# A three-layer float32 kernel: the first half batch of layer 1 multiplied with whole float32 W1out and g, their splits made later

## The chip, the core and the metric

The kernel runs on one NeuronCore of a Trainium2 chip. Its engines are called here as the profile calls them: PE (TensorE, matrix multiplications into PSUM), DVE (VectorE), ACT (ScalarE), POOL (GpSimd), SP (SyncE, which issues most of the DMA transfers). The metric is the device time of one execution in microseconds (us); lower is better.

## The reference

An approximate attention (Nystrom, 32 landmarks) feeds two gated layers; 4 batches of 576 tokens, 8 heads of 64, model width 512, inner width 2048. The weights are float64 arrays, q, k and v are float32.

```python
def _attn_ref(q, k, v):
    q_lm = q.reshape(B, H, m, S // m, D).mean(axis=3)
    k_lm = k.reshape(B, H, m, S // m, D).mean(axis=3)
    A = sm(q, k_lm)
    Bm = sm(q_lm, k_lm)
    C = sm(q_lm, k)
    Z = Bm.transpose(0, 1, 3, 2) / (norm1(Bm) * norm_inf(Bm) + 1e-06)
    for _ in range(6):
        Z = 2 * Z - Z @ Bm @ Z
    return A @ Z @ C @ v

def _moe_ref(x, w_in, w_out):
    h = x @ w_in
    g = h - np.tanh(h)
    return g @ w_out

def _moe2_ref(x, w_in, w_out):
    h = x @ w_in
    g = h * np.tanh(softplus(h))
    return g @ w_out

x = attention, heads side by side       # 2304 x 512
x = _moe_ref(x, moe_w_in, moe_w_out)
x = _moe2_ref(x, moe2_w_in, moe2_w_out)
```

## The kernel before, in words

**Products.** To keep float32 precision, an operand is kept as two float32r tiles: H, the value rounded by a copy on ACT, and L, what is left, by a subtraction on DVE or POOL (`split`). A product is then three multiplications: H with H, L with H, H with L. The attention's small products (`blocks`, `heads`) use whole float32 tiles, with several small tiles side by side in PE's array.

**Converting the weights.** A weight tile of 128x512 float64 values is loaded as 128x512x2 32-bit words into a ring of four buffers, `raw`. `f32_a` makes from the upper words a float32 y on ACT (sign, exponent and upper bits of the fraction) and moves the lower words right by 29 bits: on ACT by a Copy with a scale, or on DVE by a shift (`on_act` chooses). `f32_b` puts both together on DVE (scalar_tensor_tensor). `convert(jobs, act_share)` runs a list of such jobs as a generator, with the loads three tiles ahead; tile i shifts on ACT where i % act_share is 0. Before, the first call has act_share 1: always ACT. `keep_job` leaves a W1in tile whole (and stores it to DRAM for the later batches); `split_job` splits a tile into a buffer of `wo_p`: 16 buffers of 128x2x512, for the 16 tiles f of W1out, later of W2out.

**Slots.** Layer 1 runs over 128 slots s = 32 b + 16 hf + f: batch b, half hf of its 576 tokens (288 columns), tile f of the inner width. In `slot(s)`, `h1` makes h in PSUM by six multiplications (P, which is W1in with the attention's landmark part multiplied in by `p_gen`, times AT, the attention's left factor). `vec` takes h through ACT and DVE: s, th, q on ACT, the mask mk, products g and th, and the steps `small` and `pick` (copy_predicated) of the slot before, which finish g. Two slots later `vec` splits that g into gg (H on ACT, L on DVE or POOL). `y1` of slot s - 3 (LAG = 3) adds to four PSUM tiles y with 12 multiplications, 6 of them ahead of the background work (`bg`) and 6 behind it. After f = 15 the y tiles go out through ACT.

`E()` names the engine for the mask and the L parts: DVE, but POOL in slots 24 to 103. A scheduler orders the instructions of slots below 116 (SWITCH), with higher priority for marked ones; from there they stand as written. In the slots of batch 0, `cv` converts the rest of the first layer's weights, `p_gen` makes the next P, and `attn_all(1)` prepares the next batch. The second layer follows in 96 slots with `h2` and `o2`; its gg ring has five buffers.

Of the kernel before, what the change touches and what calls it, by code (L numbers as in the profile page):

```python
# [8 lines left out]
F32 = mybir.dt.float32  # L9
F32R = mybir.dt.float32r  # L10
# [4 lines left out]
ALU = mybir.AluOpType  # L15
# [12 lines left out]
def kernel(  # L28
# [18 lines left out]
    NF = 16  # L47
# [4 lines left out]
    PAIR = 26  # L52
    NPRE = 9
    PREP = 16
    SWITCH = 116
    C2 = 384
    NC2 = NT // C2
# [2 lines left out]

    dram = ctx.enter_context(tc.tile_pool(name="dram", bufs=1, space=DRAM))
    const = ctx.enter_context(tc.tile_pool(name="const", bufs=1))
    wo_p = ctx.enter_context(tc.tile_pool(name="wo", bufs=NF))
    st_p = ctx.enter_context(tc.tile_pool(name="st", bufs=4))
    raw_p = ctx.enter_context(tc.tile_pool(name="raw", bufs=4))
    ps_y = ctx.enter_context(tc.tile_pool(name="ps_y", bufs=4, space=PSUM))
# [24 lines left out]
    def E():  # L91

        return G if 24 <= cur[0] < NS - 24 else V

    def f32(ap):
        return ap.bitcast(F32)
# [59 lines left out]
    def split_job(src, pool, tag, dst, i):  # L156
        def done(y):
            w = pool.tile([128, 2, 512], F32R, tag=tag, name=tag)
            split(y, w[:, 0, :], w[:, 1, :], E())
            dst[i] = w  # L160
        return src, done, None

    def keep_job(src, g, j, a):
        def where():
# [11 lines left out]
    def convert(jobs, act_share=1, more=None):  # L176
        n = len(jobs)
        raws, st, los = {}, {}, {}
        ahead = 4 if more else 3

        def fetch(i):
            if i < n:
                raws[i] = load_raw(jobs[i][0], more if more and i % 6 > 3 else None)

        for i in range(ahead):
            fetch(i)
        for i in range(n + 2):
            if i < n:
                st[i], *los[i] = f32_a(raws.pop(i), i % act_share == 0)
            if i - 1 in los:  # L190
                where = jobs[i - 1][2]
                yield from f32_b(st[i - 1], *los.pop(i - 1), where() if where else st[i - 1])
            fetch(i + ahead)
            if i >= 2:
                jobs[i - 2][1](st.pop(i - 2))
            yield 1
# [345 lines left out]

    def vec(s):
        new, old = [], []
        if 2 <= s < NS + 2:
            with tc.high_priority(20):
                g2 = sv[s - 2][0]
                gg = tp[0].tile([128, 2, HS], F32R, tag="gg", name="gg")
                split(g2, gg[:, 0, :], gg[:, 1, :], E())
                sv[s - 2] = gg  # L550
        if s == NS:
            A.preload_act_table_set("mish")
            tables["prelu"] = False
        if s < NT_S:
            h = hp.pop(s)
            if s < NS:
                e = tmp(s, "s")
                t = tmp(s, "th")
                g = tmp(s, "g", 4)
                q = tmp(s, "q")  # L560
                mk = t1_p.tile([128, HS], U8, tag="mk", name="mk")
                A.activation(out=e, in_=h, func=ACTF.Square)  # L562
                A.activation(out=t, in_=h, func=ACTF.Tanh)  # L563
                with tc.high_priority(40):
                    A.activation(out=q, in_=e, func=ACTF.Exp, scale=FK)

                def mask_op(eng):
                    eng.tensor_scalar(out=mk, in0=e, scalar1=FT, scalar2=None, op0=ALU.is_ge)  # L568

                if E() is G:  # L570
                    mask_op(G)
                new = [
                    lambda: E() is G or mask_op(V),
                    lambda: V.tensor_tensor(out=g, in0=h, in1=e, op=ALU.mult),  # L574
                    lambda: V.tensor_tensor(out=t, in0=h, in1=t, op=ALU.subtract),
                ]
                with tc.high_priority(40):
                    A.activation(out=q, in_=q, func=ACTF.Square, scale=FB, bias=bias_c[:, 0:1])  # L578
                sv[s] = (g, t, q, mk)
            else:  # L580
                g = tp[1].tile([128, C2], F32, tag="g", name="g")
                gg = tp[1].tile([128, 2, C2], F32R, tag="gg", name="gg", bufs=5)
                A.activation(out=gg[:, 0, :], in_=h, func=ACTF.Mish)  # L583
                A.activation(out=g, in_=h, func=ACTF.Mish)  # L584
                new = [lambda: V.tensor_tensor(out=gg[:, 1, :], in0=g, in1=f32(gg[:, 0, :]), op=ALU.subtract)]  # L585
                sv[s] = gg
        if 1 <= s <= NS:
            g0, t0, q0, mk0 = sv[s - 1]

            def small():  # L590
                with tc.high_priority(40):
                    V.tensor_tensor(out=g0, in0=q0, in1=g0, op=ALU.mult)

            def pick():
                with tc.high_priority(40):
                    V.copy_predicated(out=g0, mask=mk0, data=t0)  # L596

            old = [small, pick]
        while old or new:
            for lst in (old, new):  # L600
                if lst:
                    lst.pop(0)()
                    yield 0
        yield 1

    def y1(s, half):
        f = s % 16
        gg = sv[s]
        w = W1o[f]
        for d in (2 * half, 2 * half + 1):  # L610
            if f == 0:
                yps[d] = ps_y.tile([128, 512], F32, tag="y", name="y")[:, 0:HS]
            c = slice(128 * d, 128 * d + 128)
            mm(yps[d], w[:, 0, c], gg[:, 0, :], start=(f == 0), stop=False)  # L614
            mm(yps[d], w[:, 1, c], gg[:, 0, :], start=False, stop=False)  # L615
        for d in (2 * half, 2 * half + 1):
            c = slice(128 * d, 128 * d + 128)
            mm(yps[d], w[:, 0, c], gg[:, 1, :], start=False, stop=(f == NF - 1))  # L618
        if f == NF - 1:
            o = raw_f32()[:, 0:2 * HS].rearrange("p (d n) -> p d n", d=2)  # L620
            for d in range(2):
                A.activation(out=o[:, d], in_=yps[2 * half + d], func=ACTF.Copy)
            nc.sync.dma_start(out=ys[s // 16][:, 2 * half:2 * half + 2], in_=o)
# [66 lines left out]
    def vec_only(g, rate=[1]):  # L690
        while True:
            yield 1
            n = 0
            for x in g:
                n += x
                if n == rate[0]:
                    break
                yield 0
            else:
                return  # L700
            yield 1
# [42 lines left out]
    if True:  # L744
# [5 lines left out]
            return [keep_job(w1i[j, g, a], g, j, a) for g in range(NG) for a in range(2)]  # L750

        def wo_jobs(src, dst, lo, hi):
            return [split_job(src[i], wo_p, "w", dst, i) for i in range(lo, hi)]

        jobs = w1i_jobs(0) + wo_jobs(w1o, W1o, 0, NPRE)
        rest = [(4 * j, n) for j in (1, 2, 3) for n in w1i_jobs(j)]
        rest += [(f + LAG, n) for f, n in zip(range(NPRE, NF), wo_jobs(w1o, W1o, NPRE, NF))]
        jobs += [x[1] for x in sorted(rest, key=lambda x: x[0])]
        rate = [1]
        cv = vec_only(convert(jobs), rate)  # L760
        pre = hi(attn_pre(0), 60)
        pa = both(attn_a, 0, 0, True)
        n = nc_ = 0
# [44 lines left out]
        def bg(s):  # L808
            b, i = s // 32, s % 32
            streams, mix = [], []  # L810
            if b == 0:
                rate[0] = 2 if i < 4 else 1
                mix.append(cv)
                while ready and i:
                    streams.append(p_gen(0, ready.pop(0)))
            if s < NS:
# [97 lines left out]
```

## Time and profile before

| what | value |
| --- | --- |
| median of 3 runs | 851.7 us (851.68 to 852.64) |
| the profiled execution | 851.59 us |
| its span in the trace | 849.8 us, 15003 instructions |
| busy, PE | 812.7 us (96%) |
| busy, DVE | 503.3 us (59%) |
| busy, ACT | 496.6 us (58%) |
| busy, POOL | 179.0 us (21%) |
| moved by DMA | 79.62 MB |

Busy shares are means over the whole span; the profile's page also has them in 40 slices of 21 us. Matmuls are pipelined, and a record lasts longer than the distance to the next: what one costs in a row of them is read from start to start. "<-" behind an idle time names what ended it. A float32 multiplication gives two records.

### The profile page before, as it was taken

The numbers are of one execution on the slowest core, as the hardware profiler recorded it, in microseconds if no ns is written. First come the engines' busy times: TensorE is split into PE (matmuls) and PEld (weight loads), VectorE is DVE, ScalarE is ACT, GpSimd is POOL, SyncE is SP. The second block draws the span as 40 slices with busy tenths as digits, with TensorE's granted clock in tenths as the row PEclk, the third lists the DMA queues.
The fourth block names the chain that finished last, engine by engine and source line by source line (L and its number), as shares of the span: only waits on it lengthen the run. The fifth ranks groups of instructions, "written<-read, shape, count | busy, mean of one in ns | idle before, by whom it ended". The sixth has DMA issues, their size and how long they took to land.

```text
span 849.8 us, 15003 instructions
## 1 busy us (share of the span) xinstructions
PE 812.7 (96%) x5656; PEld 706.5 (83%) x5656; DVE 503.3 (59%) x1158; ACT 496.6 (58%) x1234; POOL 179.0 (21%) x210
## 2 busy tenths in 40 slices
PE   4599899999999999999999999999999999999998
PEld 1346689889988899879899999999999999999996
DVE  6878999998789877999973986322111111211111
ACT  5888976788778886799874865333223222222221
POOL 0010003886577666870000000000000000000000
PEclk9557999999999999999999999999999999999999
DMA  9899240430415100360006662022002001000000
GB/s 327 289 338 366 105 136 6 148 136 1 141 51 183 51 30 1 119 215 20 29 2 225 202 195 69 1 66 74 1 1 66 10 1 49 18 1 9 30 1 37
DMA packets 34985, 79.62 MB, mean 94 GB/s; under 512 B 5472, under 2 KB 14176, under 8 KB 34912
## 3 DMA queue, kind: packets, MB, share of 16 engines
q1 hardware_dynamic: 33760, 74.46, 26.0%
q0 software_dynamic: 1152, 4.19, 1.2%
q8 instruction: 44, 0.72, 0.4%
q14 instruction: 29, 0.24, 0.1%
HBM read 65.01 MB, written 13.63 MB: 93 GB/s over the span
## 4 chain that ended last, share of the span: by engine, by line
PE 74%; DVE 12%; ACT 5%; POOL 3%; DMA 2%; issue 2%; SPq 0%; DVEq 0%; ACTq 0%
PE y L642 7%; PE y L638 7%; PE y L637 7%; PE y L614 6%; PE h L537 5%; PE h L536 5%; PE h L535 5%; PE y L618 5%; PE y L615 5%; PE m L211 3%; PE m L537 2%; PE h L511 2%; PE m L536 2%; PE m L535 2%; DVE g L596 2%; PE h L513 2%
## 5 line engine op out<-in xcount | busy, mean ns | idle before, releaser
L585 DVE TENSOR_TENSOR gg<-g,gg 128x384 fp32r<-128x384 f32 x96 | 53.5, 558 | 276.0 <-ACT g L584 276.0
L614 PE MATMUL y<-gg,w 128*128 128x288 f32 x512 | 151.3, 310 | 5.4 <-ACT gg L99 4.1
L615 PE MATMUL y<-gg,w 128*128 128x288 f32 x512 | 143.8, 296 | 0.0
L614 PEld LDWEIGHTS y<-gg,w 128*128 128x128 f32 x512 | 97.0, 189 | 29.4 <-issue 15.3
L618 PE MATMUL y<-gg,w 128*128 128x288 f32 x512 | 109.8, 299 | 1.2 <-DVE gg L100 0.8
L583 ACT ACTIVATE gg<-h 128x384 fp32r<-128x384 f32 x66 | 32.5, 492 | 132.8 <-PE h L537 132.8
L638 PE MATMUL y<-w,gg 128*128 128x512 f32 x256 | 101.2, 395 | 0.0
L637 PE MATMUL y<-w,gg 128*128 128x512 f32 x256 | 100.8, 394 | 0.0
L615 PEld LDWEIGHTS y<-gg,w 128*128 128x128 f32 x512 | 97.5, 190 | 0.0
L100 POOL TENSOR_TENSOR gg<-g,gg 128x288 fp32r<-128x288 f32 x80 | 69.3, 866 | 115.8 <-ACT gg L99 113.8
L642 PE MATMUL y<-w,gg 128*128 128x512 f32 x256 | 88.4, 396 | 0.0
L618 PEld LDWEIGHTS y<-gg,w 128*128 128x128 f32 x512 | 81.7, 189 | 6.3 <-DVE gg L100 2.1
L511 PE MATMUL h<-AT,P 128*128 128x288 f32 x256 | 79.0, 309 | 8.2 <-ACT P L490 5.1
L568 POOL TENSOR_SCALAR mk<-s 128x288 uint8<-128x288 f32 x80 | 77.7, 972 | 10.5 <-ACT s L562 4.3
L513 PE MATMUL h<-AT,P 128*128 128x288 f32 x256 | 77.7, 303 | 0.2 <-DVE P L492 0.2
L512 PE MATMUL h<-AT,P 128*128 128x288 f32 x256 | 77.8, 304 | 0.0
L596 DVE COPY_PREDICATED g<-mk,th 128x288 f32<-128x288 uint8 x128 | 74.3, 580 | 4.6
L99 ACT ACTIVATE gg<-g 128x288 fp32r<-128x288 f32 x128 | 57.1, 446 | 24.3 <-PE y L618 15.4
L578 ACT ACTIVATE q<-q,bias_c 128x288 f32<-128x288 f32 x128 | 69.1, 540 | 2.2
L574 DVE TENSOR_TENSOR g<-h,s 128x288 f32<-128x288 f32 x128 | 56.9, 445 | 19.5 <-ACT th L563 18.9
L583 ACT ACTIVATE gg<-m 128x384 fp32r<-128x384 f32 x30 | 14.8, 492 | 89.2 <-PE m L537 89.2
L562 ACT ACTIVATE s<-h 128x288 f32<-128x288 f32 x128 | 52.6, 411 | 23.9 <-PE h L513 23.8
(162 smaller groups left out, 1856.9 us busy)
## 6 DMA issues: line engine op xcount, KB each, us to landing
w<-w1s SPq DMA_DIRECT2D x24, 512.0 KB, 4.5
raw<-in_w1i_dram SPq DMA_DIRECT2D x16, 512.0 KB, 6.5
raw<-in_w1o_dram SPq DMA_DIRECT2D x16, 512.0 KB, 4.8
raw<-in_w2i_dram SPq DMA_DIRECT2D x16, 512.0 KB, 4.5
raw<-in_w2o_dram SPq DMA_DIRECT2D x16, 512.0 KB, 4.2
ys<-raw SPq DMA_DIRECT2D x16, 288.0 KB, 2.4
out_dram<-raw SPq DMA_DIRECT2D x18, 256.0 KB, 2.2
v<-in_v_dram SPq DMA_DIRECT2D x8, 512.0 KB, 8.5
```

The source lines that it names most:

```text
L100: eng.tensor_tensor(out=L, in0=src, in1=f32(H), op=ALU.subtract)
L511: mm(p, P[:, g, 0, c], AT[:, g, 0, :], start=(g == 0), stop=False)
L512: mm(p, P[:, g, 0, c], AT[:, g, 1, :], start=False, stop=False)
L513: mm(p, P[:, g, 1, c], AT[:, g, 0, :], start=False, stop=(g == NG - 1))
L568: eng.tensor_scalar(out=mk, in0=e, scalar1=FT, scalar2=None, op0=ALU.is_ge)
L596: V.copy_predicated(out=g0, mask=mk0, data=t0)
L614: mm(yps[d], w[:, 0, c], gg[:, 0, :], start=(f == 0), stop=False)
L615: mm(yps[d], w[:, 1, c], gg[:, 0, :], start=False, stop=False)
L618: mm(yps[d], w[:, 0, c], gg[:, 1, :], start=False, stop=(f == NF - 1))
L637: mm(p, gg[:, 0, cs], w[:, 0, :], start=(f == 0), stop=False)
L638: mm(p, gg[:, 0, cs], w[:, 1, :], start=False, stop=False)
L642: mm(p, gg[:, 1, cs], w[:, 0, :], start=False, stop=(f == NF - 1))
```

## The change

For the first 16 slots (NW = 16: batch 0, first half) `y1` multiplies the whole float32 W1out tile with the whole float32 g: 4 multiplications where 12 were. For these slots `vec` makes no gg. So W1out is no longer split as it is converted: `whole_job` assembles it as float32 into the first half of a `wo_p` buffer (17 now). `resplit(f)` splits tile f later, in slot 14 + f, into the next buffer: ACT copy, and a subtraction on `E()`, which is DVE for f = 0 to 9 and POOL for f = 10 to 15. `convert(jobs, 2)` lets every other tile shift its lower words on DVE. The second layer's gg ring has four buffers.

```diff
+    NW = 16
...
-    wo_p = ctx.enter_context(tc.tile_pool(name="wo", bufs=NF))
+    wo_p = ctx.enter_context(tc.tile_pool(name="wo", bufs=NF + 1))
...
+    def whole_job(src, dst, i):
+
+        def where():
+            W1f[i] = wo_p.tile([128, 2, 512], F32, tag="w", name="w")
+            return W1f[i][:, 0, :]
+
+        def done(y):
+            dst[i] = W1f[i]
+        return src, done, where
+
+    W1f = {}
+
+    def resplit(i):
+        w = wo_p.tile([128, 2, 512], F32R, tag="w", name="w")
+        A.activation(out=w[:, 0, :], in_=W1f[i][:, 0, :], func=ACTF.Copy)
+        yield 1
+        E().tensor_tensor(out=w[:, 1, :], in0=W1f[i][:, 0, :], in1=f32(w[:, 0, :]), op=ALU.subtract)
+        W1o[i] = w
+        yield 1
...
     def vec(s):
         new, old = [], []
-        if 2 <= s < NS + 2:
+        if 2 <= s < NW + 2:
+            sv[s - 2] = sv[s - 2][0]
+        if NW + 2 <= s < NS + 2:
...
-                gg = tp[1].tile([128, 2, C2], F32R, tag="gg", name="gg", bufs=5)
+                gg = tp[1].tile([128, 2, C2], F32R, tag="gg", name="gg", bufs=4)
...
         gg = sv[s]
         w = W1o[f]
-        for d in (2 * half, 2 * half + 1):
+        for d in (2 * half, 2 * half + 1) if s < NW else ():
+            if f == 0:
+                yps[d] = ps_y.tile([128, 512], F32, tag="y", name="y")[:, 0:HS]
+            mm(yps[d], w[:, 0, 128 * d:128 * d + 128], gg, start=(f == 0), stop=(f == NF - 1))
+        for d in (2 * half, 2 * half + 1) if s >= NW else ():
...
-        for d in (2 * half, 2 * half + 1):
+        for d in (2 * half, 2 * half + 1) if s >= NW else ():
...
-            return [split_job(src[i], wo_p, "w", dst, i) for i in range(lo, hi)]
+            return [whole_job(src[i], dst, i) for i in range(lo, hi)]
...
-        cv = vec_only(convert(jobs), rate)
+        cv = vec_only(convert(jobs, 2), rate)
...
+                if NW - 2 <= i < NW - 2 + NF:
+                    streams.append(resplit(i - NW + 2))
```

The scheduler places everything anew, so the order of the instructions shows more than the diff. Three places follow; the line numbers are those of the kernel that the rows belong to.

ACT before, between z (the end of the attention's iteration, which the first `p_gen` waits for) and the second copy of the first P. L131 and L137 are the two steps of `f32_a`, L99 the H copies, L490 the copy of P:

```order
L415 ACTIVATE z<-m 128x128
L99 ACTIVATE w<-y 128x512
L131 ACTIVATE y<-raw 128x512
L137 ACTIVATE raw<-raw 128x512
...
L99 ACTIVATE AT<-th 128x288
L490 ACTIVATE P<-m 128x512
L131 ACTIVATE y<-raw 128x512
L137 ACTIVATE raw<-raw 128x512
L99 ACTIVATE w<-y 128x512
L490 ACTIVATE P<-m 128x512
```

The same place of the changed kernel (L132 and L138 are `f32_a`, L511 the copy of P):

```order
L100 ACTIVATE AT<-th 128x288
L132 ACTIVATE y<-raw 128x512
L436 ACTIVATE z<-m 128x128
L132 ACTIVATE y<-raw 128x512
L138 ACTIVATE raw<-raw 128x512
L511 ACTIVATE P<-m 128x512
L132 ACTIVATE y<-raw 128x512
L511 ACTIVATE P<-m 128x512
```

Where nine conversion steps and the copy of AT stood between z and the first copy of P, two steps stand now; one stands between the two copies where three did.

PE before, a slot of the second quarter of batch 0 (L614, L615, L618 are the three kinds of y multiplication, L511 to L513 those of h):

```order
L511 MATMUL h<-AT,P 128x288
L512 MATMUL h<-AT,P 128x288
L513 MATMUL h<-AT,P 128x288
L511 MATMUL h<-AT,P 128x288
L512 MATMUL h<-AT,P 128x288
L513 MATMUL h<-AT,P 128x288
L615 MATMUL y<-gg,w 128x288
L614 MATMUL y<-gg,w 128x288
L615 MATMUL y<-gg,w 128x288
L614 MATMUL y<-gg,w 128x288
L615 MATMUL y<-gg,w 128x288
L614 MATMUL y<-gg,w 128x288
```

The changed kernel there (L636 is the whole float32 multiplication, of g itself):

```order
L636 MATMUL y<-g,w 128x288 x5
L532 MATMUL h<-AT,P 128x288
L533 MATMUL h<-AT,P 128x288
L534 MATMUL h<-AT,P 128x288
L532 MATMUL h<-AT,P 128x288
L533 MATMUL h<-AT,P 128x288
L534 MATMUL h<-AT,P 128x288
L636 MATMUL y<-g,w 128x288 x4
```

Four float32 multiplications stand between two slots' h where twelve stood, and they read g, which DVE's pick writes, without a step between.

POOL before, from slot 24 on (L100 is the L part of a split, L568 the mask, L445 a step of the next half batch's attention):

```order
L100 TENSOR_TENSOR gg<-g,gg 128x288
L568 TENSOR_SCALAR mk<-s 128x288
L100 TENSOR_TENSOR gg<-g,gg 128x288
L568 TENSOR_SCALAR mk<-s 128x288
L100 TENSOR_TENSOR gg<-g,gg 128x288
L445 TENSOR_TENSOR c<-c,xm 128x288
L568 TENSOR_SCALAR mk<-s 128x288
L445 TENSOR_TENSOR c<-c,xm 128x288
L100 TENSOR_TENSOR gg<-g,gg 128x288
```

The changed kernel there (L180 is `resplit`'s subtraction; its f = 10 to 15):

```order
L101 TENSOR_TENSOR gg<-g,gg 128x288
L591 TENSOR_SCALAR mk<-s 128x288
L180 TENSOR_TENSOR w<-w 128x512
L101 TENSOR_TENSOR gg<-g,gg 128x288
L591 TENSOR_SCALAR mk<-s 128x288
L180 TENSOR_TENSOR w<-w 128x512 x2
L101 TENSOR_TENSOR gg<-g,gg 128x288
L180 TENSOR_TENSOR w<-w 128x512
L591 TENSOR_SCALAR mk<-s 128x288
L466 TENSOR_TENSOR c<-c,xm 128x288
L180 TENSOR_TENSOR w<-w 128x512
L101 TENSOR_TENSOR gg<-g,gg 128x288
```

Five of the six subtractions stand ahead of the fourth gg (that of slot 25, when the first one is that of slot 22); the sixth follows ahead of the fifth gg.

## Rows read from the trace of the kernel before

**Rows 1.** The page's 40 slices: PE's busy tenths, and its granted clock.

```profile
PE   4599899999999999999999999999999999999998
...
PEclk9557999999999999999999999999999999999999
```

**Rows 2.** Table by stretch: start:end, length, busy time of each engine (records), clock, DMA.

```profile
40.30:71.80 31.50, 29.89 (x102) 14.11 (x103) 24.92 (x62) 25.80 (x56) 2.77 (x5) 0.55 0.94 350
71.80:117.70 45.90, 40.65 (x371) 32.94 (x370) 44.62 (x114) 40.40 (x108) 0.53 (x1) 0.99 0.42 149
117.70:138.40 20.70, 20.70 (x231) 18.90 (x224) 19.47 (x56) 15.18 (x41) 0.00 (x0) 1.00 0.44 144
138.40:163.00 24.60, 24.14 (x203) 20.71 (x203) 21.84 (x49) 19.20 (x51) 19.12 (x22) 1.00 0.15 49
```

The engines stand in the order PE, PE's weight loads, DVE, ACT, POOL.

**Rows 3.** Timeline of PE: start, duration, instruction, [idle before, and what ended it].

```profile
34.63 1.96 PE L211 MATMUL m<-w,z 64*32 64x512 f32 x16 [0.93 <-ACT z L415]
...
40.33 0.61 PE L511 MATMUL h<-AT,P 128*128 128x288 f32 x1 [3.74 <-ACT P L490]
```

**Rows 4.** Timeline of ACT, between z and the copies of P.

```profile
35.56 0.66 ACT L137 ACTIVATE raw<-raw 128x512 uint32<-128x512 uint16 x1
...
39.70 0.57 ACT L490 ACTIVATE P<-m 128x512 fp32r<-128x512 f32 x1
```

**Rows 5.** Timeline of DVE in slot 9, three steps without a gap.

```profile
89.93 0.68 DVE L100 TENSOR_TENSOR w<-y,w 128x512 fp32r<-128x512 f32 x1
90.53 0.45 DVE L574 TENSOR_TENSOR g<-h,s 128x288 f32<-128x288 f32 x1
90.90 0.44 DVE L575 TENSOR_TENSOR th<-h,th 128x288 f32<-128x288 f32 x1
```

**Rows 6.** Groups of DVE from 420 us on: the shift of lower words (busy, mean ns).

```profile
L140 DVE TENSOR_SCALAR raw<-raw 128x512 uint32<-128x512 uint32 x13 | 5.5, 422 | 0.0
```

**Rows 7.** Timeline of PE: h multiplications in a row; float32 multiplications of small tiles.

```profile
96.16 0.29 PE L512 MATMUL h<-AT,P 128*128 128x288 f32 x1
...
96.69 0.29 PE L513 MATMUL h<-AT,P 128*128 128x288 f32 x1
...
142.98 0.72 PE L211 MATMUL m<-q,kb 64*32 64x288 f32 x16
...
160.34 1.09 PE L211 MATMUL m<-w,z 64*32 64x512 f32 x16
```

**Rows 8.** Table by stretch, PE alone: its multiplications into tile y, then tile m.

```profile
71.80:117.70 45.90, 23.52 (x145) 0.99 0.42 149
...
71.80:117.70 45.90, 8.90 (x154) 0.99 0.42 149
```

**Rows 9.** Waits of PE from 71.8 to 117.7: in total us, times, longest.

```profile
PE y L614 <- ACT gg L99: 3.0, 5, 1.0
...
PE y L618 <- DVE gg L100: 0.8, 1, 0.8
```

**Rows 10.** Timeline of POOL from slot 24 on.

```profile
139.08 0.81 POOL L100 TENSOR_TENSOR gg<-g,gg 128x288 fp32r<-128x288 f32 x1 [63.54 <-ACT gg L99]
...
142.02 0.80 POOL L100 TENSOR_TENSOR gg<-g,gg 128x288 fp32r<-128x288 f32 x1 [1.11 <-ACT gg L99]
142.91 0.93 POOL L568 TENSOR_SCALAR mk<-s 128x288 uint8<-128x288 f32 x1
```

**Rows 11.** Timeline of PE: the first multiplications with L of g, slots 28 and 29.

```profile
150.62 0.43 PE L618 MATMUL y<-gg,w 128*128 128x288 f32 x2
...
154.22 0.43 PE L618 MATMUL y<-gg,w 128*128 128x288 f32 x2
```

**Rows 12.** Table by stretch, as rows 2, with stretch A cut by the clock.

```profile
40.30:58.70 18.40, 18.37 (x63) 8.85 (x64) 14.69 (x34) 15.63 (x33) 1.71 (x3) 0.50 0.87 312
58.70:62.20 3.50, 1.92 (x12) 1.45 (x11) 2.49 (x7) 2.92 (x7) 0.53 (x1) 0.97 1.03 418
62.20:72.40 10.20, 10.20 (x34) 4.41 (x33) 8.35 (x24) 7.58 (x18) 0.53 (x1) 0.51 1.05 396
```

## The prediction

> **What bounds the kernel now.** I read the page's slices first: TensorE (PE) is at 8 tenths or more from the third slice on, and its clock digits are below 9 only between 21 and 85 us [rows 1]. So whatever the change does, it does before the point from which PE runs without a break. The table by stretch shows where that lies [rows 2]. I cut it at 40.3 us, where PE starts slot 0; 71.8, slot 5; 117.7, slot 17; 138.4, slot 24, where GpSimd (POOL) takes over two of VectorE's (DVE) steps; 163.0 is about slot 32. Call the stretches A, B, C and D.
>
> A (slots 0 to 4): PE counts 29.9 of 31.5 us as busy, at a granted clock of 0.55, while DMA is at 0.94. B (slots 5 to 16): DVE 44.6 of 45.9, PE 40.7. C: PE 20.7 of 20.7, DVE 19.5. D: PE 24.1 of 24.6, POOL 19.1 [rows 2]. Behind D, PE stays at 9 tenths up to the last slice [rows 1]. Hence what is won or lost in A to D moves the end by as much, and what hangs only on ACT, or on DVE in C, counts for nothing until it passes PE.
>
> The profiled execution took 851.59 us, 0.1 from the median of the runs shown (851.7); the sum is made against 851.6. A difference under 0.2% (1.7 us) I count as none: about what a measurement of this kernel can tell.
>
> **The start of slot 0.** PE waited 3.74 us for the copy of P on ACT before its first h multiplication. The first P (p_gen) is on PE from 34.63 for 1.96 us [rows 3], but ACT, which works in order, came to its copy only at 39.70: nine conversion steps and the copy of AT stood between z and it, three more steps between the first and the second copy of P. In the change two steps stand in the first place (y and raw, 0.66 us each at most [rows 4]), one in the second. So the first copy starts when p_gen is done, at about 36.7 instead of 39.7: **-3.0 us**. It can't be more than the 3.74 us waited; it is nothing if a converted tile's DMA holds ACT up there.
>
> **Stretch A.** DVE's steps follow each other 0.60 us apart at 128x512 and 0.37 at 128x288 [rows 5]. Between slot 0's pick (copy_predicated) and slot 4's the change takes out three subtractions of gg (3 x 0.37 = 1.1) and adds four shifts and one assembly of a converted tile. A shift of that shape is in the trace later, at 422 ns, so 0.35 from start to start [rows 6]: 4 x 0.35 + 0.60 = 2.0. DVE's need rises by 0.9, from 24.9 to 25.8 us. ACT loses up to 0.66 for each shift that moves, and its copies of gg and w. If all of A's waits stay, A gives -3.0 + 0.9 = -2.1. If only DVE's need is left, it gives 25.8 - 31.5 = -5.7, and with the start -8.7. ACT, which falls most, has fewer late steps to wait for; DMA at 0.94 and the low clock stay. With nothing to choose by, I take the middle, **-5.4 us**, the start included.
>
> **Stretch B.** Here the change takes 13 gg and 7 w subtractions from DVE (13 x 0.37 + 7 x 0.60 = 9.0 us) and adds 4 shifts and 3 of the later w splits (4 x 0.35 + 3 x 0.60 = 3.2), so its need falls to 38.8 of 45.9. Then PE decides. One h or y multiplication of 288 columns takes 0.132 us (four steps in 0.53 [rows 7]); B has 145 of y and some 72 of h, 28.7 us, and the small ones into tile m are 8.9 at most: 37.6 [rows 8]. The change replaces the 145 of y (19.2 us) by 48 whole float32 ones. A float32 multiplication over the whole array is nowhere in the trace. The nearest row has eight of 64x288 side by side (16 records), done in 0.72 us; less some 0.16 of run-out (a lone record's 0.29 less 0.13) that is 0.56. The same with 512 columns is 1.09, so 0.93, or 0.52 for 288 columns [rows 7]. I take 0.53, between the two; as ends I keep 0.40 (no dearer than the three it replaces) and 0.72 (the whole row). 48 x 0.53 = 25.4, or 6.2 more: PE needs 43.8. Of its 5.2 idle us in B, 3.8 are waits for the two halves of gg, which are no longer made [rows 9]; 1.4 remain. 43.8 + 1.4 = 45.2 against 45.9: **-0.7 us**. At 0.40 DVE would bind instead (38.8 + 1.3 as now, so -5.8); at 0.72 it is +8.5. This is where the expected gain goes: DVE's 5.8 us are real, and PE grows into them.
>
> **Stretch C.** Slots 17 and 18 still multiply the last two float32 tiles: 2 x (4 x 0.53 - 12 x 0.132) = **+1.1 us**, in full, as PE has no gap there. Seven w splits come onto DVE, one a slot. With at most seven steps a slot of 0.37 or less beside it, DVE needs up to 7 x (2.6 + 0.60) = 22.4 against PE's 20.7 + 1.1 = 21.8, and less, as some steps are short. It is the next to bind, and I add nothing.
>
> **Stretch D.** The last six w splits go to POOL, in order among its gg and mk steps. POOL takes 0.81 us for 288 columns, 0.89 from start to start, and 0.93 for mk, its stretch beginning at 139.08 [rows 10]. For 512 columns I scale: by DVE's own ratio (0.68 to 0.45 [rows 5]) 1.22, by columns 1.44; I take 1.35. Walk along POOL's new order from 139.08 with gg and c 0.90, mk 1.00, w 1.35: the gg of slot 25 is done at 153.3 and that of slot 26 at 157.5. PE wants them at 150.62 and 154.22 [rows 11]. The first costs 2.7, the second, with PE that much later, another 0.6: **+3.3 us** (2.5 at 1.22, 3.8 at 1.44). PE never has time free to win it back.
>
> The Trainium skill has a smaller price for that step: "GPSIMD Engine Reference", section "3.1 Elementwise — side-by-side cycle accounting", gives some 2.6 cycles for each element of an operation with two inputs, at 1.2 GHz; as an estimate from that page 512 columns would take 0.49 us more than 288, so 1.30, D would be +3.0 and the sum 0.3 us better. Rows 10 have only the one width, 0.81 us for 288 columns or 2.8 ns each with the fixed part in it, and neither confirm nor exclude the page's slope.
>
> The rest is free. The smaller gg ring of the second layer (4 for 5) holds, because o2 of slot s-4 stands ahead of h2 of slot s on PE, and the ACT step that fills the buffer waits for h2 anyway. On SP the next batch's k and q go behind four tiles of W1in; they are wanted only in B.
>
> **Sum.** -5.4 - 0.7 + 1.1 + 3.3 = -1.7: 851.6 - 1.7 = **849.9 us**, its own range 847 to 852.
>
> **Rivals.**
> *The clock rises early (846.6, chance 0.25).* In A the clock was 0.50 (1.2 GHz) for 18.4 us in which PE had next to no gap, then 0.97 for 3.5 us of which PE worked 1.9, then 0.51 for 10.2 without a gap [rows 12], and full from 72.4. The change's first y multiplications are longer, denser and earlier, as g needs no split. If they bring the clock up in slot 1 or 2, PE is out of the way in A and DVE's need is left: -8.7 instead of -5.4. By the Trainium skill, "TensorE: Matmul & The Clock Gate", "What's actually happening", throttled is the default and activity releases it; by that rule this rival holds. Rows 12 agree only in part (18.4 busy us passed at the low clock), and no row has whole-array float32 work.
>
> *PE takes the lead and keeps its waits (856.9, chance 0.22).* In A PE was idle for 1.6 us only. If the clock stays low there, at which everything costs double, the twelve y multiplications of slots 0 to 2 add 12 x (1.06 - 0.79) = 3.2, and A gives -2.2. If in B the 5.2 us of waits stay under new names, because each g now goes straight from DVE's pick to PE, B is 43.8 + 5.2 = 49.0, or +3.1. Sum: -2.2 + 3.1 + 1.1 + 3.3 = +5.3. In B this decides from a float32 price of 0.47, where 18.4 + 48 x 0.47 + 5.2 passes 45.9. For it speaks that two engines near 95% seldom fit without gaps; against it, that 3.8 of the 5.2 were for steps that are gone [rows 9].
>
> *The loads hold A (853.2, chance 0.15).* DMA is at 0.94 in A and above 1 from 58.7 on [rows 2, 12]. If tiles land no earlier, faster conversion only waits for them: A -2.1, sum +1.6.
>
> **Numbers.** The forecast has 0.38. Its own range and the rivals put 0.45 on faster, 0.24 on within 0.2%, 0.31 on slower. With the float32 price at 0.72 the sum would be 860.6, at 0.40 843.7 (B -5.8, C 0); cutting off some of either end, the range is 844 to 858.
>
> **What would show it.** Right: the first P copy near 37 us; PE rather than DVE the busiest in B; no PE wait for gg before slot 16; slot 24 some 5 us earlier than 138.4; and behind it PE waits for POOL's gg, about 3 us. Wrong: a float32 y multiplication far from 0.53 at full clock; slot 17 before 107 or after 118; no PE wait on POOL.

## The result, and the profile after

The changed kernel takes 859.69 us (median of 4 runs, 858.52 to 860.54) against 851.69 for the kernel before in the same series; the ratio on record is 1.0081, 95% interval 1.0065 to 1.0098. (These two medians alone would give 1.0094; in the later series the kernel before has medians of 852.8 to 853.1, which give 1.008.) It is slower by 0.8%, and outside the predicted range. The profiled execution took 860.54 us; its span is 858.8 us, 9.0 more than before.

The changed kernel's page, slices of PE and its clock, against [rows 1]:

```profile
PE   4688899799999999999999999999999999999998
PEclk9578999999999999999999999999999999999999
```

The eighth slice (150 to 172 us), at 9 before, is now at 7: a hole in D. The stretches of the changed kernel cut at the same slots, against [rows 2] (PE, weight loads, DVE, ACT, POOL, clock, DMA share, GB/s):

```profile
44.20:71.80 27.60, 24.36 (x97) 12.47 (x97) 22.46 (x57) 20.80 (x46) 2.66 (x5) 0.80 0.89 304
71.80:119.60 47.80, 42.54 (x307) 29.58 (x308) 40.75 (x105) 32.32 (x87) 0.53 (x1) 0.93 0.52 187
119.60:140.80 21.20, 21.20 (x216) 18.44 (x216) 20.88 (x60) 18.08 (x48) 0.37 (x1) 1.00 0.41 136
140.80:173.20 32.40, 26.53 (x199) 20.87 (x199) 25.78 (x52) 22.23 (x58) 27.25 (x29) 0.95 0.12 43
```

B (second line) has PE, not DVE, as the busiest engine, as forecast, but 5 us of PE idle. In D PE is busy 26.5 of 32.4 us. All later readings use one measure: the start of ACT's first step (s) of a slot, the same step in every trace. Slots 24 and 32 before, then in the changed kernel:

```profile
139.35 0.41 ACT L562 ACTIVATE s<-h 128x288 f32<-128x288 f32 x1 [0.35 <-PE h L513]
...
163.32 0.41 ACT L562 ACTIVATE s<-h 128x288 f32<-128x288 f32 x1 [0.20 <-PE h L513]
```

```profile
140.82 0.41 ACT L585 ACTIVATE s<-h 128x288 f32<-128x288 f32 x1 [0.47 <-PE h L534]
...
173.15 0.41 ACT L585 ACTIVATE s<-h 128x288 f32<-128x288 f32 x1 [0.42 <-PE h L534]
```

Lengths in us:

| kernel (trace) | slot 0 at | 0 to 5 | 5 to 17 | 17 to 24 | 24 to 32 | 24 to 34 |
| --- | --- | --- | --- | --- | --- | --- |
| before | 45.6 | 27.5 | 45.7 | 20.5 | 24.0 | 31.4 |
| changed | 44.2 | 27.5 | 47.9 | 21.2 | 32.3 | 39.0 |
| predicted for it | 42.6 | 25.1 | 45.0 | 21.6 | 27.3 | |

Three traces of versions that are alike up to slot 24 (two of them are those with load added on POOL, below) have slot 0 at 41.1 to 42.6 and slot 24 at 133.3 to 134.6. So in A and B a difference under some 1.5 us between two traces says little.

### The profile page after: what moved, and what is told of

Read it like the earlier page. It is cut to its first block, busy times and chain, and to the rows that moved or that the text cites. A ratio compares the mean times of both kernels' runs of the same rounds, so it can differ in the third digit from the quotient of the medians.

```text
span 858.8 us, 14838 instructions
## 1 busy us (share of the span) xinstructions
PE 817.3 (95%) x5592; PEld 703.6 (82%) x5592; DVE 499.3 (58%) x1152; ACT 483.3 (56%) x1202; POOL 187.4 (22%) x216
## 4 chain that ended last, share of the span: by engine, by line
PE 71%; DVE 9%; ACT 7%; POOL 5%; DMA 5%; issue 2%; SPq 0%; DVEq 0%; ACTq 0%; POOLq 0%
PE y L669 7%; PE y L665 7%; PE y L664 7%; PE h L558 5%; PE h L557 5%; PE h L556 5%; PE y L641 4%; PE y L645 4%; PE y L642 3%; PE m L232 3%; PE m L558 2%; PE m L557 2%; PE m L556 2%; PE h L532 2%; PE y L636 2%; PE h L534 2%
## 5 line engine op out<-in xcount | busy, mean ns | idle before, releaser
L641 PE MATMUL y<-gg,w 128*128 128x288 f32 x448 | 131.1, 307 | 3.6 <-ACT gg L100 2.1
L642 PE MATMUL y<-gg,w 128*128 128x288 f32 x448 | 125.2, 295 | 0.0
L641 PEld LDWEIGHTS y<-gg,w 128*128 128x128 f32 x448 | 84.3, 188 | 23.8 <-issue 13.5
L645 PE MATMUL y<-gg,w 128*128 128x288 f32 x448 | 97.2, 298 | 2.9 <-POOL gg L101 2.5
L642 PEld LDWEIGHTS y<-gg,w 128*128 128x128 f32 x448 | 84.5, 189 | 0.2 <-issue 0.2
L645 PEld LDWEIGHTS y<-gg,w 128*128 128x128 f32 x448 | 71.4, 188 | 5.4 <-POOL gg L101 5.1
L585 ACT ACTIVATE s<-h 128x288 f32<-128x288 f32 x128 | 52.8, 413 | 31.9 <-PE h L534 31.9
L597 DVE TENSOR_TENSOR g<-h,s 128x288 f32<-128x288 f32 x128 | 57.0, 445 | 21.9 <-ACT th L586 21.5
L615 DVE TENSOR_TENSOR g<-q,g 128x288 f32<-128x288 f32 x128 | 63.2, 494 | 3.0 <-ACT q L601 1.7
```

## Experiments

Two theories stood at the start: that D's loss is ACT waiting for POOL, and that the gain of A and B is lost to the shifts that `convert(jobs, 2)` puts on DVE. Every ratio is the one on record, against the kernel before in the run's own series.

**ACT's wait for a buffer.** In D the changed kernel shows, among its waits (total us, times, longest):

```profile
ACT w L178 <- POOL w L180: 3.6, 3, 2.1
...
PE y L645 <- POOL gg L101: 2.5, 3, 0.8
```

`resplit(f)` writes into the buffer of tile f - 1, which POOL's subtraction still reads. The first experiment takes that away:

```diff
-    wo_p = ctx.enter_context(tc.tile_pool(name="wo", bufs=NF + 1))
+    wo_p = ctx.enter_context(tc.tile_pool(name="wo", bufs=2 * NF + 2))
...
+    def halves():
+        return [wo_p.tile([128, 512], F32R, tag="w", name="w") for x in range(2)]
```

> The changed kernel, but W1out's buffers are handed out in halves: 34 of 128x512 in place of 17 of 128x2x512 (the same memory). The whole tiles take one half, a split tile two. So the split of tile f no longer writes into the buffer of tile f - 1, from which POOL's subtraction still reads, and the copy of the next split on ACT need not wait for POOL. POOL keeps its six subtractions of w. Theory 1 (the loss in slots 24 to 31 is ACT, in order, held by that wait): slots 24 to 32, 32.3 us in the changed kernel (ACT's first step of slot 24 at 140.8, of slot 32 at 173.2), fall to the 24.0 of the kernel before plus the 3.3 that the prediction gave to POOL's load: about 27, so 859.7 - 5 = 854.5 us. Rival (POOL's load alone, each subtraction 1.28 to 1.49 us, holds gg): the slots stay at 31 to 33 us, the time at 858.5 to 860.5.

Measured: 858.11 us, ratio 1.0075 [1.0047, 1.0102]. The wait is gone from the trace. Slots 24 to 32 take 29.7 us, between the theories, but the next two give most of it back: 38.1 to slot 34, against 39.0. Not settled; a cleaner pair follows below.

**The subtractions on DVE.**

```diff
-        E().tensor_tensor(out=w[:, 1, :], in0=W1f[i][:, 0, :], in1=f32(w[:, 0, :]), op=ALU.subtract)
+        V.tensor_tensor(out=w[:, 1, :], in0=W1f[i][:, 0, :], in1=f32(w[:, 0, :]), op=ALU.subtract)
```

> The changed kernel, but all 16 subtractions of the later split of W1out are on DVE; the ring of 17 stays. Theory 1 and its rival both say that slots 24 to 32 lose POOL's part: DVE's need there is 21.8 us (before) + 6 x 0.60 = 25.4 against PE's 24.1, so 25.5 to 26.5 us where the changed kernel took 32.3: 859.7 - 6.3 = 853.4 us. If ACT's wait for the buffer is bad with any engine (DVE also works in order and comes to the subtraction late), the slots stay above 28 us and the time above 855.5.

Measured: 859.92 us, 1.0088 [1.0069, 1.0106]; slots 24 to 32 take 28.8 us and 24 to 34 36.2. Both the slots and the time fall to the second reading, a wait for the buffer that is bad with any engine; but DVE's steps have changed too. DVE's groups of this kernel, from 105 to 138 us (first fence) and, with POOL at work, from 141 to 170 us (busy, mean ns):

```profile
L180 DVE TENSOR_TENSOR w<-w 128x512 fp32r<-128x512 f32 x9 | 6.2, 684 | 0.1
```

```profile
L180 DVE TENSOR_TENSOR w<-w 128x512 fp32r<-128x512 f32 x6 | 6.4, 1070 | 0.0
...
L598 DVE TENSOR_TENSOR th<-h,th 128x288 f32<-128x288 f32 x8 | 3.5, 442 | 0.0
```

The step costs half as much again beside POOL; one that reads PSUM (th) doesn't. And from 150 to 170 us DVE (the third time in the row) has no gap left:

```profile
150.00:170.00 20.00, 17.50 (x125) 13.47 (x124) 20.00 (x40) 14.44 (x37) 14.67 (x16) 0.83 0.28 99
```

So the subtractions, taken off POOL, fill DVE instead, which would give the same miss; the pair of runs further down decides against the wait for the buffer. Behind slot 34 this trace loses 2.6 us more (slots 34 to 48 take 41.4 us, 38.8 in the changed kernel), so the execution is no shorter.

**All shifts on ACT.**

```diff
-        cv = vec_only(convert(jobs, 2), rate)
+        cv = vec_only(convert(jobs, 1), rate)
```

> The changed kernel, but the lower words of every converted tile are shifted on ACT again, none on DVE, in the first layer. Theory 2 (the gain up to slot 24 is lost because shifts that wait for a transfer stand in DVE's queue ahead of pick, so PE waits for g, and after such a wait near 82 us its clock falls): without them ACT's first step of slot 24 comes at 135 to 137 in place of 140.8, PE's granted clock stays at 1.0 between 80 and 95 us, and the time is 854 to 856. Rival (PE with float32 multiplications, or the landing of the tiles, sets the pace): slot 24 at 140 to 141.5, time 858.5 to 861. A second rival: ACT, with eight more shifts of 0.66 us, becomes late itself and slot 24 comes after 142: above 861.

Measured: 852.28 us, 0.9997 [0.9986, 1.0007], better than either theory had. Slot 0 starts at 41.9, slot 24 at 133.7 instead of 140.8, and the granted clock from 80 to 95 us is 1.00. D still takes 29.6 (37.9 to slot 34).

**The shifts alone, in the kernel before.**

```diff
-        cv = vec_only(convert(jobs), rate)
+        cv = vec_only(convert(jobs, 2), rate)
```

> The kernel before, with nothing changed but that every other converted tile of the first layer shifts its lower words on DVE. DVE was busy 44.6 of 45.9 us between 71.8 and 117.7, and the eight shifts add some 0.35 us each there and before. Theory 2: at least DVE's need, 2.8 us, and with waits for transfers in front of pick up to 6: 854.5 to 858 us. Rival (shifts on DVE cost nothing of their own, they take as much off ACT): 851 to 853.

Measured: 856.43 us, 1.0036 [1.0022, 1.0050]. The shifts cost 3.4 us there; in the trace slots 5 to 17 take 51.8 us.

**The shift issued later.** What in the shifts costs? In the changed kernel ACT, DVE and PE stand still together near 80 us. Timeline of each (start, duration, instruction, idle before):

```profile
81.80 0.69 ACT L132 ACTIVATE y<-raw 128x512 f32<-128x512 f32 x1 [2.43 <-DMA raw<-in_w1o_dram]
```

```profile
81.80 0.43 DVE L141 TENSOR_SCALAR raw<-raw 128x512 uint32<-128x512 uint32 x1 [2.10 <-DMA raw<-in_w1o_dram]
82.14 0.48 DVE L619 COPY_PREDICATED g<-mk,th 128x288 f32<-128x288 uint8 x1
```

```profile
82.67 3.89 PE L636 MATMUL y<-g,w 128*128 128x288 f32 x8 [2.03 <-DVE g L619]
```

A tile lands late; DVE waits for it at the shift, pick stands behind the shift, PE wants pick's g. And behind this gap PE's next four multiplications take 3.89 us, where the same four take 2.10 at 119.42 us; the granted clock is 0.69 from 82 to 93 us, a mean of its two levels (1.2 and 2.4 GHz).

```diff
-        else:
+        elif not one:
             V.tensor_scalar(out=lo, in0=lo, scalar1=29, scalar2=None, op0=ALU.logical_shift_right)
...
+    def f32_b(y, lo, one, late, t):
+        if late:
+            V.tensor_scalar(out=lo, in0=lo, scalar1=29, scalar2=None, op0=ALU.logical_shift_right)
+            yield 0
```

> The changed kernel, but a shift that DVE takes is issued one conversion step later, just ahead of the assembly of its tile, not behind the load. DVE does the same work; a shift that it comes to has its tile in SBUF by then. Theory 2a (what costs up to slot 24 is that DVE, in order, waits at the shift for a transfer, with pick behind it): ACT's first step of slot 24 comes at 134 to 136.5 us, as it did at 133.7 with all shifts on ACT, where the changed kernel had 140.8; DVE shows no wait for DMA over 0.5 us; the time is 853.5 to 856. Theory 2b (the shifts are plain load on DVE, wherever they stand): slot 24 at 138.5 to 141, time 857.5 to 860.5.

Measured: 859.08 us, 1.0081 [1.0049, 1.0113], slot 24 at 139.3. By the numbers this is 2b, but the run doesn't separate the two: DVE still waited 4.0 us at a shift for one W1out tile, up to 82.5 us, only at another step.

**The split begun in slot 8**, with the shifts on ACT, and with them left on DVE:

```diff
-                if NW - 2 <= i < NW - 2 + NF:
-                    streams.append(resplit(i - NW + 2))
+                if 8 <= i < 8 + NF:
+                    streams.append(resplit(i - 8))
```

> The changed kernel with all shifts of the first layer on ACT, and with the later split of W1out begun in slot 8 in place of 14, so that it ends in slot 23 and all its subtractions fall to DVE, before POOL takes part. Theory 3 (the loss from slot 24 on comes from the w subtractions there, by POOL's load, by DVE's steps with two inputs in SBUF that POOL's hold up, and by ACT's wait for the buffer): slots 24 to 32 take 24 to 24.6 us as in the kernel before (29.6 with the later split), the two-input steps of DVE there go back to the lengths of before (copy_predicated 666 ns), and the time is 852.3 - 5.5 = 846 to 848. Rival (six more subtractions of 0.6 us between slots 8 and 13, where DVE is busy 11 of 12 us, give it back earlier): slot 24 at 136 to 138 in place of 133.7, time 849.5 to 851.5.

> The changed kernel with nothing altered but the start of the later split: slot 8 in place of 14, so that it ends in slot 23 and all its subtractions are on DVE. Every other shift stays on DVE. Theory 3: slots 24 to 32 take 24 to 24.6 us where the changed kernel took 32.3, slot 24 still comes at 139 to 141.5, and the time is 851 to 853.5. Rival (DVE, with shifts and subtractions, is late between slots 8 and 16): slot 24 after 142, time 854 or more.

Measured: 846.61 us, 0.9921 [0.9906, 0.9936], with the shifts on ACT; 852.67, 1.0001 [0.9990, 1.0012], with them on DVE. Both are theory 3: slots 24 to 34 take 31.9 us in either (31.4 in the kernel before). The first is **0.8% faster than the kernel before**. Against the changed kernel's 1.0081 the shifts taken out alone give 0.84%, the late split alone 0.80%, both 1.60%: they add up. Its stretches, cut as above:

```profile
42.60:71.30 28.70, 24.84 (x98) 12.81 (x95) 22.54 (x53) 23.52 (x52) 2.66 (x5) 0.92 0.90 319
71.30:113.90 42.60, 41.10 (x311) 28.99 (x310) 40.96 (x105) 36.87 (x98) 0.53 (x1) 0.97 0.54 199
113.90:134.60 20.70, 20.70 (x202) 18.41 (x201) 20.22 (x57) 18.47 (x49) 0.28 (x1) 1.00 0.41 139
134.60:158.30 23.70, 23.59 (x211) 19.99 (x211) 21.53 (x52) 18.65 (x51) 20.04 (x22) 1.00 0.16 57
```

**Shifts on ACT and buffers in halves** (both edits above):

> The changed kernel with all shifts of the first layer on ACT, and W1out's buffers in halves (34 of 128x512), so that ACT's copy of a split needs no buffer that POOL still reads. The six POOL subtractions of w stay. With the ring of 17 the slots 24 to 32 took 29.6 us and the time was 852.3. Theory 1 (ACT's wait for POOL through the ring is most of that): 26.5 to 27.5 us, time 849.3 to 850.5. Rival (POOL's load itself, and the DVE steps that it holds up): 29 to 30 us, time 851.5 to 853.

Measured: 852.27 us, 0.9994 [0.9982, 1.0005], slots 24 to 32 30.2 us. The rival holds; the wait for the buffer costs nothing of its own. Theory 1 falls. Nor is D's loss the clock's: in the changed kernel's D the granted clock is 0.95, but this trace has it at 1.00 and still takes 38.4 us from slot 24 to 34:

```profile
133.40:171.81 38.41, 32.24 (x258) 26.42 (x257) 29.97 (x66) 25.89 (x72) 33.29 (x35) 1.00 0.25 86
```

**Early and late shifts.** Of the 32 tiles, shifts on DVE only from the seventeenth on, or only before it (split from slot 8):

```diff
-                st[i], *los[i] = f32_a(raws.pop(i), i % act_share == 0)
+                st[i], *los[i] = f32_a(raws.pop(i), i % act_share == 0 or (act_share == 2 and not more and i < 16))
```

> As the version with the split begun in slot 8, but of the 32 tiles only those from the seventeenth on shift on DVE, every other one (8 tiles, converted from about 42 us on); the first sixteen shift on ACT. All on ACT gave 846.6 us, every other of all 32 gave 852.7. If the harm is done in the slots (DVE waiting in front of pick): 851 to 853. If it is done before slot 0, where late shifts keep the raw buffers and so the loads back (13.0 MB loaded at 45 us with DVE's shifts, 13.6 without): 846.5 to 848.5. Between: each does its part.

> The counterpart: only the first sixteen tiles shift on DVE, every other one (8 tiles, converted before some 42 us); all later ones on ACT. Harm in the slots: 846 to 848. Harm before slot 0, by the loads that come later: 850.5 to 853, with under 13.3 MB loaded at 45 us.

Measured: 850.27 us, 0.9968 [0.9953, 0.9984], late ones only; 849.21, 0.9957 [0.9940, 0.9974], early ones only (`i >= 16` in the diff). Against 846.61 that is 3.7 and 2.6 us, together 6.3, near the 6.1 of all sixteen: each half does its part. With the early ones fewer bytes are loaded by 45 us. From the start to 45 us, DVE busy, clock, DMA share and GB/s of the early-split kernel with no shifts on DVE, with late ones, with early ones:

```profile
0.00:45.00 45.00, 30.14 (x82) 1.00 0.89 299
```

```profile
0.00:45.00 45.00, 30.76 (x83) 0.69 0.90 303
```

```profile
0.00:45.00 45.00, 30.86 (x85) 1.00 0.86 292
```

That is 13.5, 13.6 and 13.1 MB (the changed kernel: 13.0). There is little room to catch up: DMA's share is 0.99, 1.06 and 0.85 in the changed kernel from 60 to 72, 82 and 93 us.

**The next batch's loads later**, on either version of the early split:

```diff
-                if i == 3:
+                if i == (3 if b else 6):
...
-                if i >= 5:
-                    streams.append(gens["a"])
+                if i >= (5 if b else 9):
+                    streams += [gens["a"]] * (2 if b == 0 and i < 13 else 1)
```

> As the version with all shifts on ACT and the split begun in slot 8 (846.6 us), but the next batch's k, q and v (3.5 MB, which stand in SP's queue ahead of the last seven W1out tiles, while DMA is at 0.94 to 1.07 from 60 to 90 us) are loaded in slot 6 in place of slot 3 in batch 0, and that batch's attention starts in slot 9 in place of 5, with two parts for one in slots 9 to 12. Theory 4 (transfers set the pace from 60 to 95 us with either kind of shift): W1out's last tiles land up to 8 us earlier, slots 8 to 10 come 2 to 4 us earlier, the time is 842.5 to 845. Rival (with shifts on ACT nothing waits for transfers any more; DVE's and PE's steps set the pace): 846 to 848.

> The same later loads of k, q and v, with every other shift on DVE and the split begun in slot 8 (852.7 us with the loads in slot 3). Theory 4 (a shift on DVE hurts because DVE, in order, waits there for a tile that the full DMA queues deliver late, near 66 and 82 us): without the late tiles DVE waits under 1 us for DMA between 60 and 100 us, PE's waits for g near 82 us go, and the shifts on DVE cost at most 2.5 us against the same kernel with the shifts on ACT: 845 to 848.5. Rival (the shifts are steps in DVE's chain of pick and assembly, whatever the loads do): 5 us or more against it, 850 to 853.5.

Measured: 848.21 us, 0.9949 [0.9935, 0.9964], and 851.42, 0.9980 [0.9964, 0.9995]. Slot 10 starts at 83.3 instead of 89.4, and at 87.4 instead of 93.9. But slots 11 to 15, into which the attention is packed, give it back (22.6 us for 15.4 in the first version), and that version ends slower, just above the ranges of both theories. That transfers set the pace up to slot 10 isn't shown. With the loads in slot 3 and the shifts on ACT no engine waits for a DMA from 72 to 100 us; ACT converts no tile from 70 to 80 us and five in slots 8 and 9, where it is busy 10.0 of 10.2 us, and one there with the later loads. But the attention's steps left slots 5 to 8 as well, and the two aren't separated. The shifts on DVE cost 3.2 us here, 0.31% by the ratios, about half of the 6.1: between the two theories. A gentler placing (loads in slot 5, attention from slot 8, made up in slots 18, 20 and 22; the same lines with these numbers):

> As the version with all shifts on ACT and the split begun in slot 8, with the next batch's k, q and v loaded in slot 5 in place of 3 in batch 0, its attention begun in slot 8 in place of 5, and the three slots made up by two parts for one in slots 18, 20 and 22 (in the earlier try they were made up in slots 9 to 12: slot 10 came 6 us earlier, but slots 11 to 15 took 7 us longer). Theory 4 (transfers hold slots 5 to 10, and the earlier try lost the gain to the attention packed into slots 9 to 12): slot 24 at 130.5 to 133 in place of 134.6, the time 843 to 845.5. Rival (PE, which has no gap from 93 us on, has the same work to do, and the time saved comes back as PE time): slot 24 at 134 to 136, the time 846 to 848.5.

Measured: 852.41 us, 0.9998 [0.9985, 1.0010]. Slot 10 comes at 85.7, but slots 15 to 18 take 13.6 us for 7.5 and 24 to 34 36.9 for 31.9. Also a miss, slower than both theories had: the gain up to slot 10 isn't kept this way either.

**POOL's time, or what its reads do to DVE?** POOL load added to the version with early split and shifts on ACT, in slots 24 to 31, without and with SBUF reads:

```diff
                 if E() is G:
+                    if 24 <= s < 32:
+                        for x in range(5):
+                            G.memset(mkw, 0.0)
                     mask_op(G)
```

(or, for the three added lines' inner two, `G.tensor_tensor(out=mkw, in0=w[:, 0, 0:224], in1=w[:, 1, 0:224], op=ALU.subtract)` twice, with w the split tile s - 16. The buffer mkw, 128x224 float32, takes the place of the mask's own in these slots; that edit isn't shown.)

> As the version with all shifts on ACT and the split begun in slot 8 (846.6 us; slots 24 to 34 took 31.95 us in its trace), but with load added on POOL that writes and reads nothing: in slots 24 to 31 five memsets of 128x224 ahead of each mask, into the mask's own buffer. I count on about 1.2 us a slot for the six slots from 26 on. Theory 5a (POOL's time alone, gg and mk coming late, makes the loss of slots 24 to 34): 36 to 39 us for these slots, the time 850 to 854. Theory 5b (a POOL step that reads SBUF holds up DVE's steps with two inputs in SBUF, copy_predicated and small, and these make the loss): copy_predicated stays under 600 ns there, the slots at 32 to 34 us, the time 846 to 849.

> The same place and about the same POOL time (1.2 to 1.4 us a slot), but two subtractions of 128x224 with both inputs in SBUF in place of the five memsets; their result is not used. 5a: the same loss as with the memsets, within 1 us. 5b: copy_predicated goes to 680 ns or more and small above 500, slots 24 to 34 take 36 to 39 us, the time is 850 to 854, and at least 3 us longer than with the memsets.

Measured: 854.13 us, 1.0021 [1.0008, 1.0034], with memsets; 854.58, 1.0026 [1.0012, 1.0041], with subtractions. Groups of DVE and of POOL from 134 to 170 us, with memsets (first two fences) and with subtractions:

```profile
L626 DVE COPY_PREDICATED g<-mkw,th 128x288 f32<-128x288 uint8 x8 | 4.0, 500 | 2.8 <-POOL mkw L595 2.7
```

```profile
L600 POOL MEMSET mkw<- 128x224 f32 x30 | 8.6, 286 | 1.3
```

```profile
L627 DVE COPY_PREDICATED g<-mkw,th 128x288 f32<-128x288 uint8 x8 | 5.1, 637 | 1.8 <-POOL mkw L595 1.7
```

```profile
L601 POOL TENSOR_TENSOR mkw<-w 128x224 f32<-128x224 f32 x12 | 8.8, 731 | 1.2 <-DVE g L627 0.4
```

POOL's added time is the same, 8.6 and 8.8 us; copy_predicated takes 500 ns with the memsets, 637 with the subtractions and 562 in the version with neither; and slots 24 to 34 take 39.0 and 38.9 us. So 5a: POOL's own time is enough for the loss, and what its reads do to DVE adds nothing in these slots. (Four of the sixteen subtractions ran before slot 24; there DVE has no gap, and slots 17 to 24 take 21.5 us for 20.7.) Slots 24 to 34 without the added load and with memsets, POOL the fifth time in the row:

```profile
134.63:166.58 31.95, 30.82 (x270) 26.06 (x269) 28.81 (x69) 23.63 (x64) 26.11 (x29) 1.00 0.30 104
```

```profile
133.30:172.29 38.99, 33.46 (x270) 27.17 (x269) 28.55 (x69) 23.75 (x65) 32.63 (x59) 0.96 0.24 85
```

POOL's idle time there goes from 5.8 to 6.4 us: the added work used none of it.

**The kernel before, once more:**

> The kernel before, unchanged, for another trace of it. Its first trace begins with a granted clock of 0.50 up to 56 us; the traces of the experiments (the one of the kernel before with shifts on DVE among them) begin at 1.00. If the low clock holds stretch A, slot 5 comes at 69 to 71.5 us here in place of 73.2 and the execution is 2 us or more shorter. If loads and conversions hold it whatever the clock, slot 5 comes at 72 to 73.5 and the time is 850 to 853.

Measured: 850.93 us (one execution). The first trace of this kernel, too, has its clock at 1.00 up to 18 us; the 0.50 holds from there to 58 us. Here the clock is full up to 80 us. The first trace, then this one:

```profile
20.00:58.00 38.00, 29.13 (x274) 14.21 (x275) 31.56 (x78) 33.07 (x71) 2.25 (x4) 0.50 0.85 300
```

```profile
20.00:58.00 38.00, 28.82 (x274) 13.56 (x273) 31.93 (x79) 32.50 (x70) 2.27 (x4) 1.00 0.85 294
```

Slot 5 comes at 71.2 (73.2 before), but slot 24 at 138.7 against 139.4: of what the low clock costs in A, 0.6 us is left by then. By slot 5 the first reading holds, by the time the second.

## Why the prediction was wrong, by its own steps

| step | predicted | changed | early split, shifts on ACT |
| --- | --- | --- | --- |
| start of slot 0 | -3.0 | -1.4 | -3.1 |
| rest of A | -2.4 | 0.0 | +1.2 |
| B | -0.7 | +2.2 | -3.1 |
| C | +1.1 | +0.7 | +0.2 |
| D, to slot 32 | +3.3 | +8.4 | -0.4 |
| sum | -1.7 | +9.8 | -5.1 |

The steps are differences to the first trace of the kernel before, by ACT's s. By the forecast's own mark for the start, PE's first h, the changed kernel begins 2.0 us earlier (38.37 for 40.33 [rows 3]).

**Two steps failed.** The first is D. "Walk along POOL's new order" let POOL use its idle time. Its work was sized rightly: 27.25 us busy in D against 19.12 [rows 2], 8.1 more, which is six times the 1.35 taken (single ones took 1.28 to 1.49). The estimate of 1.30 by the Trainium skill, "GPSIMD Engine Reference", section "3.1 Elementwise — side-by-side cycle accounting", agrees too. But POOL's idle time did not shrink: 24.6 - 19.1 = 5.5 us before, 32.4 - 27.25 = 5.2 now. POOL's timeline shows it:

```profile
143.03 1.28 POOL L180 TENSOR_TENSOR w<-w 128x512 fp32r<-128x512 f32 x1 [0.50 <-ACT w L178]
...
148.46 1.45 POOL L180 TENSOR_TENSOR w<-w 128x512 fp32r<-128x512 f32 x1 [0.74 <-ACT w L178]
149.87 0.79 POOL L101 TENSOR_TENSOR gg<-g,gg 128x288 fp32r<-128x288 f32 x1
...
163.88 0.67 POOL L478 TENSOR_TENSOR c<-c,xm 128x288 f32<-128x288 f32 x1 [1.19 <-ACT q L588]
```

POOL's gg releases PE, which, in order, makes the next h behind it; h releases ACT's s, and s POOL's mask and, later, gg. The waits in that ring stay, and work added to it comes on top. The walk charged only two late gg; what late masks and attention steps (c) hold up was left out. PE did wait 2.5 us for POOL's gg in D, near the 3 that the forecast named, but it was idle for 5.9. That this ring is the reason is read from the order of the steps; that POOL's added time alone makes the loss, the memsets show: 8.6 us of them, 7.0 us longer.

The second is the shift, priced as "0.35 from start to start" of DVE's need and only from slot 0 on: 2.8 us in A and B, in B even hidden under PE. The sixteen cost 6.1 to 7.2 us, the early eight, charged with nothing, 2.6 of it. With all on ACT the start of slot 0 is -3.1, as forecast. What part is plain load on DVE (sixteen times 0.42 us is 6.7), what part waiting for tiles and what part the lower clock behind such waits stays open: moving the next batch's loads halved the cost, but moved the attention too.

**Two errors hid each other.** The float32 multiplication was taken at 0.53 us. The changed kernel has at full clock:

```profile
105.81 2.59 PE L636 MATMUL y<-g,w 128*128 128x288 f32 x10
...
109.02 1.62 PE L636 MATMUL y<-g,w 128*128 128x288 f32 x6
```

Two multiplications (four records) more make 0.97, so 0.485 each. With that the prediction's own sum gives B 18.4 + 48 x 0.485 + 1.4 = 43.1 us; the version with shifts on ACT took 42.6. Against it A was forecast too short, a third term that was wrong (-2.4, where 0.0 was measured): even with the shifts on ACT it is 1.2 us longer than before, with the loads 1.4 MB behind at 65 us (19.4 to 20.8 MB). And against the second trace of the kernel before, in which the clock was full, nothing is left of the early start by slot 5: it comes at 71.3 and 71.2.

**What would show it.** The first P copy came at 37.72, against 39.70 [rows 4] and the 36.7 forecast:

```profile
35.97 0.67 ACT L132 ACTIVATE y<-raw 128x512 f32<-128x512 f32 x1 [0.35 <-DMA raw<-in_w1o_dram]
36.55 0.65 ACT L138 ACTIVATE raw<-raw 128x512 uint32<-128x512 uint16 x1
37.72 0.60 ACT L511 ACTIVATE P<-m 128x512 fp32r<-128x512 f32 x1 [0.52 <-PE m L232]
```

ACT waited 0.52 us for p_gen, which ends a microsecond later than before [rows 3]. PE the busiest in B, and no PE wait for gg before slot 16: right. Slot 17, at 118.5 by PE's first h (119.6 by ACT's s), lies just past the 118 that was to count as wrong, and slot 24 came 1.5 us later, not 5 earlier.

**The rivals.** The clock did rise early (0.80 in A against 0.55), and gave next to nothing: the kernel before at full clock gains 0.6 us by slot 24. "The loads hold A", at 0.15, fits that A gained nothing, and ACT did wait 3.4 us there for W1in's tiles; but so it did in the second trace of the kernel before, and no run moves these loads alone. "PE takes the lead and keeps its waits" came nearest in time (856.9) with B 47.9 against its 49.0, but not for its reason: its waits in B came with the shifts and went with them.

## What to carry to other kernels

Idle time of an engine inside a ring of dependences (here POOL, ACT, PE) is not room: charge work added there nearly in full (by slot 34, 0.8 to 0.94 us for each us here), not by what exceeds the idle time. Small steps moved to an engine whose queue holds the next product behind them can cost all their busy time, though it has gaps in the mean (here 6.1 to 7.2 us for 6.7); where such a step may wait for a transfer, try it on the engine that has to wait for that transfer anyway. When a change is several edits, price and test each alone: here the large edit was worth 0.8%, and two small ones beside it lost twice that.

## What the runs showed of the hardware

DVE's steps with two inputs in SBUF take longer when POOL steps that read SBUF run beside them. copy_predicated takes 483 ns without POOL, 500 with memsets added to POOL's work, 637 with subtractions; small 452, 517 and 607; the w subtraction 684 without POOL and 1070 beside it; th, with an input in PSUM, 447 and 442. By the Trainium skill, "SBUF — State Buffer", section "Who interferes with whom", a VectorE instruction with two SBUF inputs contends with a GpSimd instruction that reads SBUF, not with one that only writes it: the traces agree on both points. It cost no time in slots 24 to 34 with load added on POOL, where DVE wasn't the one waited for; with the subtractions on DVE there was no gap on it from 150 to 170 us, and there it counts.

The granted clock isn't set by the program alone: from 20 to 58 us the same kernel before shows 0.50 in one trace and 1.00 in another, with PE busy 29.1 and 28.8 us, at 849.8 and 849.1 us of span.
